# Linear attention and a two-layer ELU network: key projections in 64-row pairs over four banks, zero matmuls in the ramp's gaps, other planned load times and a new fixed order

## The chip, the cores and the metric

One core of one Trainium2 chip. The time is the device time of one launch in microseconds (us); lower is better. A kernel is run several times, and two kernels that are compared run in turn on the same chip. A run that is more than 1.5% above the fastest of the same kernel in its batch is called slow: medians and ranges below include such runs, ratios leave them out. "Span" is the time from the first to the last instruction of one profiled execution; the device time is some 1.8 us longer.

Engines: TensorE does matmuls and transposes, ScalarE the exponentials, VectorE maxima and sums, GpSimd the scaling of the values; GpSimd also issues most of the loads. "Granted clock" is the share of its full clock that the throttle gave TensorE.

## The reference, cut to what matters

```python
# q, k, v: (8 batches, 8 heads, 576 positions, 64); w_phi: (64, 128)
def phi(x):
    proj = einsum('bhsd,df->bhsf', x, w_phi)
    proj = proj - max(abs(proj), axis=-1, keepdims=True)
    return concatenate([exp(proj), exp(-proj)], axis=-1)

q_p, k_p = phi(q), phi(k)
kv  = einsum('bhsf,bhsd->bhfd', k_p, v)
z   = sum(k_p, axis=2)
x   = einsum('bhsf,bhfd->bhsd', q_p, kv) / (einsum('bhsf,bhf->bhs', q_p, z)[..., None] + 1e-6)

x = x.transpose(0, 2, 1, 3).reshape(4608, 512)
h = x @ w_in                                     # w_in: (512, 2048)
g = where(h > 0, h, exp(minimum(h, 0)) - 1)
return g @ w_out                                 # w_out: (2048, 512)
```

## The kernel before

The kernel handles four heads of a batch at a time (a "quad"; 16 in all). For each quad it transposes keys and queries, projects them with `w_phi`, takes exponentials, forms the key-value product (`pkv`), multiplies the queries into it (`pn`), divides, and passes `x` on to the two layers (`ph` is the hidden layer, `po` the output layer). The layers are by far the larger part of TensorE's work.

Nothing is looped in program order. All steps are put down as operations with a cost in us, what they depend on, and how many PSUM banks they take. A planner plays the program through on paper and emits each engine's instructions in the order in which its model started them. What goes first among the ready ones is set by a table of fixed ranks, found by search. So the order is fixed when the kernel is built, and it is as good as the model's numbers are.

The keys before, one step for each bank, on all 128 rows (two 64-row halves beside each other, `w_phi_rhs` is block-diagonal):

```python
def project(n, hh, bank):
    pk = psum(bank, [P, 4, F], FP32, "pk")
    for j in range(2 if hh < 4 else 1):
        nc.tensor.matmul(
            pk[:, 2 * j:2 * j + 2, :].rearrange("p a b -> p (a b)"),
            in_tile(n)[:, 2 * hh + j, :],       # weights
            w_phi_rhs,                          # 128 rows x 256 columns, half of it zeros
            start=True, stop=True)
# ... (cut)
for hh in range(5):
    bank = Bank("first")
    # ... (the exponentials, cut)
    o = add({"PE": 0.22 if hh < 4 else 0.11},
            lambda e, hh=hh, bank=bank: project(0, hh, bank), ..., new=[bank], ...)
```

The queries were already done in the way that the keys get now: two matmuls on 64 rows each, side by side in the array, into two banks.

```python
def project_halves(n, c, pair):
    pk = [psum(bank, [P, 4, F], FP32, f"pk{par}") for par, bank in enumerate(pair)]
    for j in range(4):
        for par in range(2):
            r = slice(par * D, (par + 1) * D)
            nc.tensor.matmul(pk[par][:, j, :], in_tile(n)[r, 4 * c + j, :],
                             w_phi_both[r, par, :], start=True, stop=True)
```

The planner's model of the ramp, and how it gave out banks:

```python
COLD = 20.0            # until then TensorE's costs count times COLD_TIMES
COLD_TIMES = 1.2
CHANGE = 0.095         # a change between 128-row and 64-row matmuls
# ... (cut)
bank.index = min(banks)
```

Of the kernel before, what the change touches and what calls it, by code (L numbers as in the profile page):

```python
# [34 lines left out]
    "020F0U0V0c0a0X0f0b0j0i1E1u1I0l1g1q1o4X3h0n3M3W4j594k580L3J0A01162V4W2W0Z3R0h1U0Y"  # L35
    "2F0+0I1B0Q0-0g560P071b0q181Z0x1y2I0J0T3V1H1p0H381n0S3u1e4z5W3K2M2U323+D9355+4p1J"
    "0E552Z1j0v3700Cp0m3X152S3w0d3r3j061s3p2q6c2m1c453A3H4H0y2O2N0o0N280e1r200M3E4b2n"
    "2r1x0W1t2s1a1l2K0R09121+19102d0k0C2f1z2e11364y2R7n0w535c5g5m313l1X3Y808E8B4V469B"
    "5a5j71C75r6y1k8J2Q42033m0D1CES5D0K9V0G1Y2p1f1S8u4B048V5n4a4c8b3d3B2x5O2P5X0B4I5K"
    "6d9c5M508l0rA3246W1L512cB08zBm30278+AJ2h6e146l3T3e7-5B25E184394D6bAm9-8FEW936j1D"  # L40
    "9Y82AH5q6a8r2y0OEH13I67e9a79B92Y6I5dCC659ICJ8iDy7u4MAGDe9ZB5DGBoErBxFpD+E4DTD5AK"
    "GQDuDl3C3x4Y4A3N263I3OAc235y433U9J3PAN1N8y3yEj4F6R2D1v8Z1A1T225CD7A58K8N5-3ZA-7I"
    "BN773t1Q0p2X8s5s4x4U1w1O1-7z4qAf8j1R2b8e2J6B2z6T3G5Q9M3-5E8Y055N343n3oDp3D6F2l4o"
    "4887215b1G8M4L1F4Z3sBz2w081W5S9z4+3Q7r409u4u6S4e6m1h9v3k4ED4AE4J4s447L4f5p2HA72i"
    "7X7m1dDhB+By2CDD9E4i5T4m6f2B6J7N7Y4R7l9U49Bu9yBL9d5P0uCD5V5H2-BRAY9D6OB-FU4O5F9A"
    "BpA19X3g3L6q4T3i4l880s4G9r4tBk2uDqAsA+3F6o9q5oAq647qCK4w5i2EFF336Q66Iz8W8c8OK98n"
    "J+5fPN2tEq7UPM5e6XAtDi9SBa9pJy1P607THX9RA08AIY2v8d90IOBVE2A4IPB1JE5ZI9ASFo8xBqDz"
    "GjECEuEeE6KcDbQX7vHJFAJgHTEMFRFrEADsN84g543f5A5k6n3q3c6g5w4Q8o6h8U740z2G4h6-6L1m"
    "1i6N3zCt9t7w2A9P3a7VEK6kC-9TD37P8hCPBF8L7SBd8DAe8RCdEZ6z6s8kBT8SCxDA707i7M7Z6Z41"
    "B27fDK635h5I4CCcE0Fq949FBbBI8T6rCb81BeCa8XCOH84-9KDc5Y4N9b6Y0t7E6D2+9h3b17C96A6E"  # L50
    "C49G2j7OCy7j8I4d8G992gDM6V1M97291K6p734P6+2L8QE5EPBD8C9xAxCY9kC81V5z7R7CAwDF4r4S"
    "8t962k5vAADJFGH35JG4B6CsG-62CeEnCRBlM+BA8wCQ52DtC0AhAF5LF8CI6tAPI0Bs6M86CEEE687g"
    "HvEBHO5lPeF0GuALKgDOKxAvKLBvH0AdFMFDIF7ABOCkG+83IDDV8p91QPAgHBAUDgEOH27yApFSHI85"
    "HmCL7B9QO8FjDnD0ITFLLs6uMJJwDRN-FBEyHWLOGJHDNUMMHSH9G6I2FsNAHMIxD-674n3SAi7aBi4K"
    "EmBBDrB372D1CgBQ78BZ9O6iABGKBg75CF9wG9B7EhCzAR8fEsB4AbBM7G69BHCN7sJoCjLWCo4vF+G1"
    "F2ClCvAlFeJpJmGx6CEtCV9HDHC3An8v2o9LL2MXELOJDSEYNnFmDNN7GkDvJhHyG3J49WETEJ47Ex6K"
    "DmBK615R9eAyGnA89iD2DECw6GF96P6HGUEk92Bj95CuCrDxFYC2FnBEFCF47KGOCX9mD8BJAzBXFHCZ"
    "AOA67pHiBSF3EV5tCSCTCMDUG5ChC1BULpGgE+K-DkEpHKGYDYMy7xH6HaJlFzAVBtHCFdHREwFwPUGc"
    "C5AoH+G7L67oPTEFIV5GKVHEM47kLoHQIo7FFkCWFcBrJHDLLaN1ICIRF6H-JuJDM17hRmHqL-FiIXIn"
    "L889LxIwK7AZKPIMLrAkG8JILVGwHVKhKI7dIUP3NFPREvJaLmPuSsQqPWLFHxNhQ7MQElOSMLSwPAQc"  # L60
    "GWI8HHAr2a9N6vFWGm3v9g8PGVFXCAE7CHF7E-7tCfDdEf5xAQF5A2E9FuFT8gGHGAEcDXCnG0BwFf76"
    "BGFyGz6wGrGPGCGIKi7DCUGqCBEiLcFIGDKZFtGXBhAuFlEIHdFVJ7HLMmH1EdNEGZHeNdOIDaOECGHj"
    "N5DoGiIsKeG2Ge9sEN57AIGG8mLNDCGdBY985uF1IgIcCqGaJrLDGRGS6xFx9l9oCmGpEGFPH7FaLI8H"
    "GfBnGv7QAMHGGNAWBcGs8aD6GLHfFZNpLZNwLGLtHFIZGEFhI-DfHZJeIyJnV3I1NbI5JSMuL5JdLuOQ"
    "EaAjH4HYKWP8J8BfHbJfKyIuKDMqMOFJIiJ3Jk9jJLIeM0IqHAE8IKJWPJM5Q4AXT0NXSI7WPXKRTPDI"
    "HzHkJAIWOUJzKkIaKoL+LfJCO6KAJO9CRkJtTS8qLvJjJFLjHUJqIhAaPSQQQ2PfSAPDMHOzPEQfM3S0"
    "OsOlO2P9NLNgNtRRRwPjPpQFOT6U5UDZ9n7bFbGBF-DwK1KBC+ACKUIpKYKrKzKEH5ISLdJKLJP0JQJJ"
    "KsQBLRLKHrKTJ2IrOpN3CiEXC6HhJTQj9+GyI4ItKjJRLXKqKlIEJ5DQL0MBN4JXJZIQOHJ6RnMpNYGF"
    "K+PBJbMnNiHpMGREMKI+SnBPMZK2IIMDMoDWDjEQEgL4INQwKNJGDBOPQmJNL9PzKSJsERHoKtKJIbGt"
    "KXS7QzJBFEFKHcJ9J1NMLAKbJUDPQAEDK3KmMdJVL3K8NzLHO4QMNqQuOGKGLMMYNkKMS3IAQyLzHnOc"  # L70
    "TyIBNmR6J0POMrI7R2IfLUNTMsNCODOyLCHlP5QiLn7JKHNxLEJPJ-NrX47cPdNPMFFNOKRBMlEbIGNj"
    "K59fLyOjWW7+UQPFMN8-U3MTVGGbUpMjWeHtLqPhWcIHILQeWpOmPPPiTVL7GTRHVtA9KnPgX1LlUKPQ"
    "RZQhPKQ8NSPlSuTdT9SoHsV6VKWGVsRAPaU2VBThXOQCOkB8BWGhBCMROgGoK0MkNRO7S4S8SbN0QNJi"
    "QxObOwJcSBNKS5TxOCOeLTTwSJTvU8O1V2R5U9V7LYROT-UoIlT7JvLkO0QLUcIjW5S6MtOONuP6RWRS"
    "JxQbSNLwOMOYNaKfR0MPMfPCMWMhSpMgM2P7M8NOQSUzNvQGO9PmP+FgMvE3EUQUKKLPP2OFKuKdQ6QO"
    "MVV+KpMiJYOqLLOvTEL1SCLeLbV4NZMcSqVXRNOLKwPqIkQERaSzOXKaQHImEzEoTDKQOfLiNGTKPrOo"
    "OhQpOWQsO3RpVpWBRjSxVSRTXGVbR1VmTRRPN9TzRgQ3R7R-NJSyWSJMHNTgXKQ5OdTJTFQRPxRCWJMU"
    "I3QKW+LSTLRuWoOiUgOZPtMaHgSeQ-RDU4ShWqXJUfNoXILhNeVcX8WPSmRtVYP1OASiRMW6TjTQWXO-"
    "U0StWxTGUbSRXLSaUnTnWFWCTeR+PVTcWHVVRIUTOVWDVdVOSTRLUYTBUEV9WaSkONFQFvMSIvVjVgNN"
    "RzMANlMEPySQSGMzSFQrOxSVK6SKSfSgPsSEW0RyT2RsUPKCPkS1NWTuW4RxVxIJS2NVM7RXNyQZVZQY"  # L80
    "GlM6SDVlQ0QTGMUITbQtQWSdOrRQMeMbNcSlUWVTQnWuVUQ1V-VQOuVEVLPIXNTkUCMxKFLgTWSZT4SS"
    "R9U-OBLBO5UAPwNHUXU6P-K4TIRoN6T5SHRfM-QJKvRJN2VhT+SWRlORRbRYLQQaReM9NfOaT3RiRdRV"
    "NBMCTiTmSPViP4QvVPUkNDN+SrV5PvScW2WLPcXDVoTXWAWIPbW7WRSLSjWQVwNQVJULUiSYXEMIU+Rv"
    "VqTsUMR4WgOtHwQdWjIdUOS+VIPGURTMX6WwKOPoX5FOUrTrWtX9TlR3WmUvUqUhX2WVUtV0TUWfVaQk"
    "WzUdUZTfWbSXUmRrWkMwU5RUXCWdUwSOWTWrTZUsVMWZRqSUTATYUuTpPZUyQlVvTCUGQ9UxUaT8W1WM"
    "VyVCPLRcX7NsUVRGW-7HPHVkXFQVUJT6WlWvW3UHWNVHUBS-XAO+U7TtWyATVrV8X0WsUSR8X3UeVDVu"
    "TTXQUDVfXHVFUUVWW9WhW8RFWUQoUNV1XMXPUFTqWiPnWnVRXBU1UjVNVAWKTHSvWORKT1ToPYUlQgTO"
    "VnVeQ+QDOnRhWYSMWETNVzQITa2THPADHuNIS9"
# [37 lines left out]
class Planner:  # L126
# [4 lines left out]
    COLD = 20.0  # L131
    COLD_TIMES = 1.2
# [9 lines left out]
    def __init__(self):  # L142
        self.ops = []
        self.slot = 0.0

# [22 lines left out]
    def run(self):  # L168
        free = dict.fromkeys(self.LAG, 0.0)
        ready = {e: [] for e in self.LAG}  # L170
        banks = set(range(8))
# [61 lines left out]
        while todo:  # L233
            started = False
            for e in ready:
# [22 lines left out]
                for x in o.cost:  # L258
                    ready[x] = [y for y in ready[x] if y[1] is not o]
                for bank in o.new:  # L260
                    bank.index = min(banks)
                    banks.remove(bank.index)
                    held[bank.kind] += 1
                    left[bank.kind] -= 1
                    moe[0] = moe[0] or bank.kind == "ph"
# [4 lines left out]
                if e == "PE" and now < self.COLD:  # L270
                    c *= self.COLD_TIMES
# [17 lines left out]
            for o in [o for o in pending if o.seen <= now]:  # L289
                pending.remove(o)  # L290
                for bank in o.new + o.uses:
                    bank.users -= 1
                    if not bank.users:
                        banks.add(bank.index)
                        held[bank.kind] -= 1
                        started = True
# [13 lines left out]
def kernel(  # L310
# [151 lines left out]
    def plan_quad(i):  # L462
# [32 lines left out]
        for n in range(2):  # L495
# [4 lines left out]
            if i >= DMA_QUAD:  # L500
# [6 lines left out]
                def tail_by_dma(e, n=n, t0=t0):  # L507
# [5 lines left out]
                    {"SP": 1.27}, by_dma, [main, *prior], key=-4.0, load=0.5, alone=1.85  # L513
# [3 lines left out]
                    load=0.15, alone=1.1,  # L517
# [77 lines left out]
        for hh in range(5):  # L595
            bank = Bank("first")


            def exp_k(e, sg, s=None, hh=hh, bank=bank):
                r = slice(0, P) if s is None else slice(s * TAIL, (s + 1) * TAIL)  # L600
                n = 4 if hh < 4 else 2
                nc.scalar.activation(  # L602
                    EK()[:, hh, sg, :] if hh < 4 else EKt[r, s, sg, :],
# [5 lines left out]
            o = add(  # L609
                {"PE": 0.22 if hh < 4 else 0.11},  # L610
                lambda e, hh=hh, bank=bank: project(0, hh, bank),
                [moved[0][0 if hh < 4 else 1], *old("kv")],
                new=[bank],
                key=first + 0.1 * hh if i != 1 else 0.35 + 0.01 * hh,
            )
            ops["k"].append(o)
            m_k.append(
                add(
                    {"DVE": 0.6 if hh < 4 else 0.34},
                    lambda e, hh=hh, bank=bank: reduce(  # L620
                        0,
                        slice(hh // 2 * NS + hh % 2 * NT, hh // 2 * NS + hh % 2 * NT + NT)
                        if hh < 4
                        else TAIL_COLS,
                        bank,
                    ),
# [5 lines left out]
            for sg, s in (  # L632
                ((0, None), (1, None)) if hh < 4 else ((0, 0), (0, 1), (1, 0), (1, 1))
# [3 lines left out]
                        {"ACT": 0.48 if hh < 4 else 0.27},  # L637
# [503 lines left out]
    for c in range(2):  # L1141
        nc.sync.dma_start(out=wst[c * D:(c + 1) * D, :], in_=w_phi)
# [12 lines left out]
    for _ in range(9):  # L1155
        nc.tensor.matmul(warm, zeros[:, 0:P], zeros[:, 0:CHUNK], start=True, stop=True)  # L1156
# [103 lines left out]
```

## Time and profile before

| | before |
|---|---|
| median of 3 runs | 378.59 us (377.31 to 378.9) |
| the profiled run | 375.57 us, span 373.8 us, mean granted clock 0.966 |
| first hidden-layer matmul | 52.9 us |
| TensorE from 10 to 60 us | busy 39.3 of 50 us, granted clock 0.51 to 0.94 |
| ScalarE from 10 to 60 us | busy 47.4 of 50 us |

The profiled run was a lucky draw, 3 us under the median. Single runs of this kernel went from 375.6 to 382.9 us over the whole study, and to 385.4 with the slow ones, so only means of several runs on the same chip are compared below. The table is read as two parts. From the first hidden-layer matmul on, TensorE is full, and the end comes a nearly fixed time later. Before it is a ramp in which loads and four engines share the pace. The lines that carry this stand in the prediction.

### The profile page before, as it was taken

The numbers are of one execution on the slowest core, as the hardware profiler recorded it, in microseconds if no ns is written. First come the engines' busy times: TensorE is split into PE (matmuls) and PEld (weight loads), VectorE is DVE, ScalarE is ACT, GpSimd is POOL, SyncE is SP. The second block draws the span as 40 slices with busy tenths as digits, with TensorE's granted clock in tenths as the row PEclk, the third lists the DMA queues.
The fourth block names the chain that finished last, engine by engine and source line by source line (L and its number), as shares of the span: only waits on it lengthen the run. The fifth ranks groups of instructions, "written<-read, shape, count | busy, mean of one in ns | idle before, by whom it ended". The sixth has DMA issues, their size and how long they took to land.

```text
span 373.8 us, 8380 instructions
## 1 busy us (share of the span) xinstructions
PE 354.6 (95%) x3095; PEld 194.5 (52%) x3095; DVE 267.6 (72%) x558; ACT 274.8 (74%) x604; POOL 247.9 (66%) x359
## 2 busy tenths in 40 slices
PE   6686789999999999999999999999999999999995
PEld 3464664565455654555545546554555554444443
DVE  5789888896897877868875899687978653647000
ACT  3999899899988775986699899977795524656111
POOL 8998959899479558795735871795278733646000
PEclk9578889999999999999999999999999999999999
DMA  8999995999228996589865833761030212000223
GB/s 106 237 252 207 203 179 64 201 190 210 65 49 127 241 209 91 75 133 193 132 77 151 142 55 74 198 168 33 28 89 2 60 43 77 0 30 0 85 61 82
DMA packets 85785, 43.15 MB, mean 115 GB/s; under 512 B 54704, under 2 KB 79664, under 8 KB 85744
## 3 DMA queue, kind: packets, MB, share of 16 engines
q1 hardware_dynamic: 56416, 26.62, 32.5%
q0 software_dynamic: 29328, 16.00, 30.6%
q8 instruction: 24, 0.39, 0.4%
q14 instruction: 17, 0.14, 0.1%
HBM read 36.77 MB, written 9.44 MB: 124 GB/s over the span
## 4 chain that ended last, share of the span: by engine, by line
PE 82%; ACT 9%; DVE 4%; POOL 2%; issue 2%; ACTq 0%; POOLq 0%
PE po L1078 31%; PE ph L1012 29%; PE pkv L783 5%; ACT EK L602 4%; PE pn L831 4%; PE pk L556 4%; PE pk L574 2%; PE tr L528 2%; PE pq L700 2%; ACT EKt L602 1%; ACT Eq L751 1%; PE warm L1156 1%; DVE gT L1035 1%; DVE m_k L583 1%; PE pnt L846 1%
## 5 line engine op out<-in xcount | busy, mean ns | idle before, releaser
L1078 PE MATMUL po<-w_out_sb,gT 128*128 128x512 bf16 (+1 forms) x592 | 136.4, 373 | 0.1
L1028 POOL TENSOR_SCALAR u_sb<-e_sb 128x512 bf16<-128x512 f32 x144 | 88.3, 620 | 55.7 <-ACT e_sb L1024 50.2
L1035 DVE SCALAR_TENSOR_TENSOR gT<-u_sb,ph 128x512 bf16<-128x512 bf16 x144 | 96.1, 683 | 40.1 <-POOL u_sb L1028 39.3
L1012 PE MATMUL ph<-xT,w_in_sb 128*128 128x512 bf16 x512 | 119.3, 379 | 0.8 <-DVE gT L1035 0.7
L1024 ACT ACTIVATE e_sb<-ph 128x512 f32<-128x512 f32 x144 | 86.4, 611 | 38.4 <-PE ph L1012 35.3
L1012 PEld LDWEIGHTS <-w_in_sb 128*128 128x128 bf16 x576 | 54.4, 98 | 63.5 <-issue 4.1
L1078 PEld LDWEIGHTS <-gT 128*128 128x128 bf16 x592 | 55.0, 98 | 57.1 <-issue 4.3
L670 POOL TENSOR_TENSOR vs<-v_b,em 128x512 bf16<-128x512 f32 (+1 forms) x96 | 78.1, 840 | 0.1
L602 ACT ACTIVATE EK<-pk 128x512 bf16<-128x512 f32 x128 | 70.2, 621 | 9.0 <-PE pk L556 7.7
L751 ACT ACTIVATE Eq<-pq 128x512 bf16<-128x512 f32 x128 | 68.4, 614 | 3.4 <-PE pq L700 3.2
L583 DVE TENSOR_REDUCE m_q<-pk 128x4 f32<-128x512 f32 (+1 forms) x80 | 47.8, 629 | 13.0 <-PE pk L574 9.2
L583 DVE TENSOR_REDUCE m_k<-pk 128x4 f32<-128x512 f32 (+1 forms) x80 | 48.5, 631 | 4.1 <-PE pk L556 3.0
L909 POOL TENSOR_TENSOR x<-tot,rec 128x576 bf16<-128x576 f32 x28 | 31.9, 1150 | 16.0 <-DVE rec L905 11.9
L1101 ACT COPY o_sb<-po 128x512 f32<-128x512 f32 (+1 forms) x27 | 15.5, 573 | 35.7 <-PE po L1078 34.4
L866 DVE TENSOR_TENSOR tot<-pn,w 128x260 f32<-128x260 f32 x64 | 26.7, 424 | 8.5 <-PE pn L831 6.3
L831 PEld LDWEIGHTS <-Eq 128*128 128x128 bf16 x512 | 22.9, 98 | 10.4 <-DVE tot L872 1.4
L872 DVE TENSOR_TENSOR tot<-tot,pn 128x260 f32<-128x260 f32 x64 | 26.5, 420 | 0.7
L783 PEld LDWEIGHTS <-EK 128*128 128x128 bf16 x512 | 23.8, 102 | 4.2 <-PE pq L700 0.7
L831 PE MATMUL pn<-kv,Eq 128*128 128x65 bf16 x512 | 25.4, 195 | 0.5 <-DVE qT L536 0.2
L556 PE MATMUL pk<-w_phi_both,kT 128*128 128x256 bf16 x144 | 24.5, 281 | 1.1 <-ACT kv L797 0.4
L602 ACT ACTIVATE EKt<-pk 64x256 bf16<-64x256 f32 x64 | 23.6, 380 | 2.6 <-PE pk L556 2.0
L783 PE MATMUL pkv<-vs,EK 128*128 128x65 bf16 x512 | 25.2, 200 | 0.2 <-DVE m_q L583 0.2
(74 smaller groups left out, 296.2 us busy)
## 6 DMA issues: line engine op xcount, KB each, us to landing
out_dram<-o_sb SPq DMA_DIRECT2D x32, 256.0 KB, 2.5
v_b<-in_v_dram SPq DMA_DIRECT2D x6, 1024.0 KB, 6.4
k_b<-in_k_dram POOLq DMA_DIRECT2D x7, 512.0 KB, 8.1
q_b<-in_q_dram POOLq DMA_DIRECT2D x7, 512.0 KB, 8.7
w_in_sb<-in_moe_w_in_dram POOLq DMA_DIRECT2D x8, 256.0 KB, 7.8
w_out_sb<-in_moe_w_out_dram POOLq DMA_DIRECT2D x4, 512.0 KB, 15.1
v_b<-in_v_dram POOLq DMA_DIRECT2D x2, 512.0 KB, 6.4
v_b<-in_v_dram POOLq DMA_DIRECT2D x1, 1024.0 KB, 11.9
```

Of the source, the lines that this page charges most:

```text
L556: nc.tensor.matmul(pk[:, 2 * j:2 * j + 2, :].rearrange("p a b -> p (a b)"), in_tile(n)[:, 2 * hh + j, :], w_phi_rhs, start=True, stop=True,)
L583: nc.vector.tensor_reduce(largest(n)[:, cols], bank.tile[:, 0:len(range(2 * NS)[cols]), :], axis=AX.X, op=ALU.max, apply_absolute_value=True,)
L602: nc.scalar.activation(EK()[:, hh, sg, :] if hh < 4 else EKt[r, s, sg, :], bank.tile[r, 0:n, :].rearrange("p a b -> p (a b)"), ACT.Exp, sc ...
L670: nc.gpsimd.tensor_tensor(st["vs"][:, sg, r, 0:D], kqv[b, 2][:, o:o + n * D].rearrange("p (n d) -> p n d", d=D), st["em"][:, sg, r, None]. ...
L751: nc.scalar.activation(dst, src, ACT.Exp, scale=1.0 - 2.0 * sg)
L783: nc.tensor.matmul(pkv[:, c, sg, :], st["EK"][:, 2 * c + s, sg, t * F:(t + 1) * F] if t < NT else EKt[:, s, sg, c * F:(c + 1) * F], st["vs ...
L831: nc.tensor.matmul(pt[:, t, :], st["Eq"][:, par, c, sg, o:o + P], st["kv"][:, s, c, sg, :], start=True, stop=True,)
L1012: nc.tensor.matmul(ph, w_in_sb[:, ct, jt * P:(jt + 1) * P], xTs[ch][:, ct, :] if ch < B else xT_tail[:, ct // 2, :, ct % 2, :], start=(ct ...
L1024: nc.scalar.activation(t["e"], bank.tile, ACT.Exp)
L1028: nc.gpsimd.tensor_scalar(t["u"], t["e"], -1.0, 1.0, op0=ALU.add, op1=ALU.mult)
L1035: nc.vector.scalar_tensor_tensor(gTs[ch][:, jt, :], t["u"], 0.0, bank.tile, op0=ALU.min, op1=ALU.max)
L1078: nc.tensor.matmul(bank.tile, gTs[ch][:, jt, tt * P:(tt + 1) * P], w_out_sb[:, jt, o0:o1], start=(jt == 0), stop=(jt == N_JT - 1),)
```

## The change

Its intent: the keys' projection wastes half the array on zeros; the clock is low in the ramp because TensorE has holes there; and the plan's load times don't fit. The diff, without the rank table (all of which is new):

```diff
-    COLD = 20.0
-    COLD_TIMES = 1.2
+    FILL_UNTIL = 60.0
+    FILL = 0.056
@@ the planner starts an operation
+                if e == "PE" and 0.0 < free[e] and now < self.FILL_UNTIL and banks:
+                    n = int(0.5 * (now - free[e]) / self.FILL)
+                    if n:
+                        if filled not in banks:
+                            filled = min(banks, key=banks.get)
+                        self.fill(filled, n)
                 for bank in o.new:
-                    bank.index = min(banks)
+                    bank.index = min(banks, key=lambda j: (j == filled, banks[j], j))
@@ the transposing DMAs (main, tail), for keys and queries and for x
-                    load=0.5       load=0.15
+                    load=0.7       load=0.22
@@ the keys
-        for hh in range(5):
-            bank = Bank("first")
+        main_banks = [[Bank("first") for _ in range(2)] for _ in range(2)]
+        tail_bank = Bank("first")
+        def keys(e):
+            for c in range(2):
+                project_halves(0, c, main_banks[c])
+        for new, c in (((*main_banks[0], *main_banks[1]), None), ((tail_bank,), 2)):
+            o = add({"PE": 0.11 if c else 0.44}, ..., new=new, mode=0 if c else 1, ...)
     (exponentials, maxima and the key-value product use the new order of the rows)
@@ divide
-            den = tile("den", small, [P, 2 * NS], FP32)
+            den = small.tile([P, 2 * NS], FP32, name="den", bufs=2)
@@ the start
-    for _ in range(9):
-        nc.tensor.matmul(warm, zeros[:, 0:P], zeros[:, 0:CHUNK], start=True, stop=True)
+    fill(7, 30)      # thirty 128-column matmuls of zeros
```

## The prediction

> **What bounds the kernel now.** I read the slices of the span first, then stretches of ten and twenty microseconds, then the waits of TensorE, then the chain of waits, and last the order of instructions around single steps.
>
> The slices (each digit is the busy share in tenths of a fortieth of the span, 9.35 us):
>
> ```profile
> PE   6686789999999999999999999999999999999995
> ACT  3999899899988775986699899977795524656111
> POOL 8998959899479558795735871795278733646000
> PEclk9578889999999999999999999999999999999999
> ```
>
> TensorE is full from the seventh slice on and at the full clock. Before that it has holes and a granted clock well below full, while ScalarE and GpSimd are full. So there are two parts: a ramp to about 57 us, and a part in which TensorE alone sets the pace. The stretches put numbers to it (per engine: busy us and instruction count; then the clock, the DMA share and GB/s):
>
> ```profile
> core 0: us, PE busy (x) PEld busy (x) DVE busy (x) ACT busy (x) POOL busy (x), PEclk, DMA share, GB/s
> 10.00:20.00 10.00, 7.13 (x52) 4.99 (x52) 7.28 (x15) 9.67 (x26) 9.55 (x15) 0.51 1.33 231
> 20.00:30.00 10.00, 8.77 (x132) 6.39 (x131) 8.91 (x20) 9.55 (x26) 9.98 (x15) 0.81 1.25 247
> 30.00:40.00 10.00, 6.83 (x85) 4.54 (x85) 9.44 (x21) 9.82 (x25) 8.94 (x13) 0.70 1.31 207
> 40.00:50.00 10.00, 7.04 (x117) 6.13 (x115) 9.03 (x23) 8.74 (x20) 6.35 (x9) 0.84 1.32 187
> 50.00:60.00 10.00, 9.53 (x96) 5.85 (x93) 7.70 (x18) 9.61 (x21) 9.13 (x15) 0.94 1.26 168
> ...
> 200.00:220.00 20.00, 20.00 (x206) 11.02 (x205) 16.08 (x35) 16.92 (x37) 13.30 (x20) 1.00 0.60 129
> ```
>
> From 10 to 60 us TensorE is busy 39.3 of 50 us, so 10.7 us are idle. Busy time times (1 - clock), row by row, gives 3.5 + 1.7 + 2.0 + 1.1 + 0.6 = 8.9 us that it worked longer than at full clock. ScalarE is busy 47.4 of the same 50. From 60 us to the last matmul at 369.5 us TensorE idles about 0.6 us in all (0.11, 0.05, 0.24 and 0.20 in four stretches). A microsecond of TensorE work taken out there comes off the time one for one; one taken out of the ramp does so only where TensorE is what the others wait for. The chain of waits (start, us, what) shows where that is:
>
> ```profile
> 10.92 1.87 PE tr L528 x16
> 12.78 1.41 PE pk L556 x6
> ...
> 19.85 1.71 PE tr L528 x16
> ...
> 38.01 2.36 PE pkv L783 x40
> ...
> 48.39 2.20 PE pkv L783 x40
> ...
> 202.28 1.26 PE pkv L783 x40
> ```
>
> The same 40 matmuls of the key-value product take 2.36 and 2.20 us in the ramp and 1.26 later: the throttled clock lies on the chain.
>
> **What the Trainium skill says.** "TensorE: Matmul & The Clock Gate", Part 1, says the clock is halved by default, that a sustained busy window of about 3.4 us releases it, and that an idle one takes it back. The trace agrees in kind: the mean clock is 0.51 from 10 to 20 us and 1.00 when TensorE is full. Nothing in this trace says how full a window must be, which is the open point about filling half a gap. The same page, Part 3 "Packing small matmuls", says that matmuls on different row groups run at the same time. "TensorEngine Tiling", "Key Properties", says that changing the tiling mode drains TensorE. Both can be measured in a query step, which is already in 64-row pairs:
>
> ```profile
> 161.68 0.29 PE L783 MATMUL pkv<-vs,EK 128*128 128x65 bf16 x4
> 161.80 0.19 PE L783 MATMUL pkv<-vs,EKt 128*128 128x65 bf16 x1
> 161.93 0.40 PE L574 MATMUL pk<-w_phi_both,qT 64*128 64x128 bf16 x8
> 162.16 0.38 PE L700 MATMUL pq<-qT,w_phi_both 64*128 64x512 bf16 x2
> 162.47 1.90 PE L1078 MATMUL po<-w_out_sb,gT 128*128 128x512 bf16 x8
> ```
>
> Eight 64-row matmuls take 162.16 - 161.93 = 0.23 us, so a pair takes 0.058. Groups of five key-value matmuls start 0.158 apart, so the next thing could have started at 161.84; it started at 161.93, 0.09 later. The two wide ones take 0.216 (the pitch of a 512-column matmul), to 162.38; the next starts at 162.47, again 0.09. A change of mode is thus 0.09 us, two per isolated step. "TensorEngine Tiling", Gotcha 1, adds that row tiles running together need different PSUM banks, which is why the new key step takes four banks at once; query steps of this kernel do so already.
>
> **The change part by part.**
>
> 1. Keys. Now: eight 256-column matmuls per quad at 0.107 us (five of them in the full-clock part span 0.71 us with a last one of 0.27, so (0.71 - 0.27)/4 = 0.11), 0.86 us. After: sixteen 64-row, 128-column matmuls in eight pairs at 0.058, 0.46 us. Saved 0.40 per quad; two changes of mode cost 0.18 where the step stands alone, none where it lies beside a query step. Net 0.22 to 0.40. After 57 us the trace has 102 key matmuls, nine to a quad, 11.3 quads. So 11.3 x 0.22 = 2.5 to 11.3 x 0.40 = 4.5 us; I take 3.0, because a step that needs four free banks will seldom be placed right beside another that needs four. The ScalarE, VectorE and key-value counts don't change: the other order of the rows is only followed by other indices.
>
> 2. Zeros in the gaps. The old warm-up of nine 512-column matmuls (4.0 us) becomes thirty of 128 columns; at half clock 30 x 0.107 = 3.2 us, and the first keys land at 5.5 us either way. In the ramp, half of each planned gap is filled at 0.056 per matmul. If the planned idle is like the measured 10.7 us, that is some 5.3/0.056 = 95 matmuls plus a few before 10 us (an estimate). At half clock the same number takes about the whole gap, so TensorE would look full until the clock is released and half full in its gaps after that. I expect the clock from 10 to 60 us to rise from about 0.76 to 0.9 or more. The chain's throttled pieces then shrink: key-value 1.10 + 0.94, transposes 16/16/8 by about 0.9 + 0.8 + 0.4, keys 0.6: 4.7 us. That is the most the clock alone can give. ScalarE has only 50 - 47.4 = 2.6 us of idle in the stretch, so when TensorE gets out of the way ScalarE is next. Of 4.7 I take half, 2.4 us.
>
> 3. Banks are now given out longest-free first rather than lowest number first. That removes some waits for a bank's last reader in the ramp (transposes waited 2.4 us for ScalarE and 1.2 us for VectorE there), though most of these are for data or a true lack of banks. Counted in point 2.
>
> 4. Longer planned transposing DMAs, no planned cold factor, new ranks. No instruction changes its cost by these; only the order does. After 57 us there is nothing to gain in order, since TensorE idles 0.6 us. In the ramp a plan that fits the clock better is worth perhaps 1 us, in the sum. Against this, bursts of four banks of keys (eight exponentials of ScalarE, some 4.5 us to drain) leave less room for the hidden layer: I add back 0.3 us.
>
> Sum: 3.0 + 2.4 + 1.0 - 0.3 = 6.1 us, and from a median of 378.6 that is 372.5. As these new ranks were presumably kept because they paid, I shade it to 372.0 us, 1.7% faster.
>
> **The rivals.**
>
> Rival A: the ramp is ScalarE's and GpSimd's. For it: both are over nine tenths busy through most of 10 to 60 us, and the DMA engines are past their share as well (1.25 to 1.33). Then the warm clock only turns slow TensorE work into idle TensorE time, and all that is left is the keys after 57 us: 378.6 - 3 = 375.6. Against it: the throttled key-value products are on the chain with their full 2.36 and 2.20 us.
>
> Rival B: a shorter latency starts the hidden layer earlier, and everything after gains. The first hidden-layer matmul starts at 52.9 us, right after the copy of the second quad's transposed output. If the chain's 4.7 us come through whole and the new order adds 2, the gain is 3.5 + 4.7 + 2 = about 10 us, 368.5. For it: TensorE has nothing useful to do before that start. Against it: ScalarE's 2.6 us of slack.
>
> Rival C: the new step takes with one hand what it gives. Four banks at once starve the hidden layer of banks, zeros are in the way of real work that comes early, and the fixed order stalls. Then holes of 0.1 to 0.5 us appear in the full part and the time is 376 to 380. Against it: thirty-two query steps of four banks run in the full part today with almost no hole.
>
> **The range and the chances.** A gives 375.6, my sum 372, B 368.5, C above 376. The range 368 to 376 leaves a tenth to each side. The line for faster by over 2% is 378.6 x 0.98 = 371.0, just 1 us below my figure. With a spread of about 3 us I give 0.40 to faster, 0.57 to within, and 0.03 to slower, which only C in a bad form reaches.
>
> **What would show each step right or wrong.** Keys: in the full part, a key step of sixteen matmuls should take 0.46 us start to end with 0.09 before and after; TensorE's work after the ramp should be some 3 us shorter. If the pair's pitch is 0.1 or the change of mode more than 0.09, step 1 is wrong. Clock: the rows from 10 to 60 us should show 0.9 or more, and the first key-value products about 1.3 us; if the clock stays at 0.7 to 0.8, half a gap isn't enough. Ramp: the first hidden-layer matmul should start 2 to 3 us earlier than 52.9. If it starts at 52 or later with a warm clock, A is right; if before 48, B. Idle of TensorE after 60 us should stay under 1.5 us; more means C. The prediction falls if the new order changes what is done in the ramp so much that the start of the hidden layer moves by more than 5 us either way.

## The result, and the profile after

| | before | after |
|---|---|---|
| median | 378.58 us (4 runs, 377.31 to 378.9) | 373.62 us (4 runs, 372.9 to 374.2) |
| span of the profiled run | 373.8 us | 372.0 us |
| mean granted clock in it | 0.966 | 0.995 |
| first hidden-layer matmul | 52.9 us | 51.5 us |

The ratio is 0.9874 [0.9846, 0.9903], 1.3% faster, or 4.8 us of 378.6. A ratio here is the mean time of one kernel's fast runs over that of the other's in the same rounds, so it isn't quite the ratio of the medians; the brackets hold its 95% interval.

The slices after:

```profile
PE   7786988999999999999999999999999999999995
PEclk9999899999999999999999999999999999999999
```

The clock is 9 tenths or more in every slice but the fifth (8), where the second to the sixth were 5, 7, 8, 8 and 8 tenths. The rows of ten microseconds from 10 to 60 us, in the columns that the prediction explained:

```profile
10.00:20.00 10.00, 7.48 (x110) 5.76 (x109) 8.25 (x17) 9.53 (x24) 8.49 (x13) 1.00 1.35 212
20.00:30.00 10.00, 8.77 (x165) 6.79 (x165) 7.97 (x15) 9.93 (x27) 9.31 (x15) 1.00 1.17 192
30.00:40.00 10.00, 6.93 (x124) 5.68 (x121) 8.04 (x20) 6.90 (x19) 9.04 (x13) 0.87 1.21 231
40.00:50.00 10.00, 8.56 (x145) 7.25 (x143) 9.19 (x23) 9.61 (x23) 9.63 (x12) 0.96 1.35 207
50.00:60.00 10.00, 9.84 (x110) 5.31 (x110) 8.22 (x18) 9.57 (x22) 8.86 (x15) 1.00 1.40 224
```

The clock averages (1.00 + 1.00 + 0.87 + 0.96 + 1.00)/5 = 0.97, with its lowest row at 0.87. But TensorE's busy time is no less than before, since zeros are counted as work, and the hidden layer starts only 1.4 us earlier. The chain of waits says what the ramp is made of now (start, us, what):

```profile
5.54 7.16 DMA k_b<-in_k_dram
...
25.17 10.60 DMA q_b<-in_q_dram
...
36.90 1.69 PE pkv L797 x40
...
45.71 3.54 ACT EK L629 x7
...
50.20 13.69 DMA k_b<-in_k_dram
```

Three loads account for 31 us of the first 64 us of this chain. Only one long piece of the key-value product is left on it there. The waits of TensorE (total us, times, longest) agree:

```profile
PE tr L537 <- DMA k_b<-in_k_dram: 2.5, 2, 1.2
PE trt L541 <- DMA q_b<-in_q_dram: 1.9, 1, 1.9
```

The new key step stands here between two parts of the output layer:

```profile
77.52 1.03 PE L1097 MATMUL po<-w_out_sb,gT 128*128 128x512 bf16 x4
78.49 0.62 PE L583 MATMUL pk<-w_phi_both,kT 64*128 64x128 bf16 x16
79.04 3.63 PE L1097 MATMUL po<-w_out_sb,gT 128*128 128x512 bf16 x16
```

Four wide matmuls at a pitch of 0.216 end at 78.38 and the keys start at 78.49. From there to the next matmul it is 0.55 us: eight pairs at 0.058 make 0.46, and the change of mode makes 0.09. (The 0.62 of the record runs to the modelled end of the last matmul.) From one output part to the next it is 79.04 - 77.52 = 1.52 us. And the zeros:

```profile
L1247 PE MATMUL fill<-zeros 128*128 128x128 bf16 x212 | 20.4, 243 | 3.1 <-DVE zeros L1163 1.0 <-DVE tot L885 0.9 <-ACT EK L629 0.6
```

212 matmuls, 30 at the start and 182 in gaps. At a pitch of 0.056 those in the gaps fill some 10 us.

### The profile page after: what moved, and what is told of

It is laid out like the page before. It is cut to its first block, busy times and chain, and to the rows that moved or that the text cites. A ratio compares the mean times of both kernels' runs of the same rounds, so it can differ in the third digit from the quotient of the medians.

```text
span 372.0 us, 8975 instructions
## 1 busy us (share of the span) xinstructions
PE 352.5 (95%) x3380; PEld 197.1 (53%) x3426; DVE 266.9 (72%) x562; ACT 271.8 (73%) x601; POOL 248.3 (67%) x359
## 4 chain that ended last, share of the span: by engine, by line
PE 76%; DMA 8%; POOL 6%; ACT 4%; issue 3%; DVE 1%; POOLq 0%; ACTq 0%
PE po L1097 33%; PE ph L1031 27%; DMA k_b<-in_k_dram 6%; PE pkv L797 4%; PE pk L583 4%; PE pn L850 3%; DMA q_b<-in_q_dram 3%; POOL u_sb L1047 2%; POOL vs L684 2%; PE pq L714 1%; ACT EK L629 1%; POOL w_in_sb L385 1%; PE pnt L865 1%; ACT EKt L629 1%; DVE gT L1054 1%
## 5 line engine op out<-in xcount | busy, mean ns | idle before, releaser
L1097 PE MATMUL po<-w_out_sb,gT 128*128 128x512 bf16 (+1 forms) x567 | 130.8, 373 | 1.6 <-issue 0.6
L1047 POOL TENSOR_SCALAR u_sb<-e_sb 128x512 bf16<-128x512 f32 x144 | 88.0, 618 | 49.4 <-ACT e_sb L1043 46.4
L1031 PEld LDWEIGHTS <-w_in_sb 128*128 128x128 bf16 x576 | 53.6, 98 | 62.0 <-issue 4.2
L1097 PEld LDWEIGHTS <-gT 128*128 128x128 bf16 x592 | 54.0, 98 | 56.9 <-issue 2.9
L629 ACT ACTIVATE EK<-pk 128x512 bf16<-128x512 f32 x128 | 68.6, 628 | 11.9 <-PE pk L583 11.5
L765 ACT ACTIVATE Eq<-pq 128x512 bf16<-128x512 f32 x128 | 69.9, 622 | 3.2 <-PE pq L714 3.1
L891 DVE TENSOR_TENSOR tot<-tot,pn 128x260 f32<-128x260 f32 x64 | 25.7, 420 | 0.4
L797 PEld LDWEIGHTS <-EK 128*128 128x128 bf16 x512 | 22.3, 98 | 3.3 <-PE fill L1247 0.2
L797 PE MATMUL pkv<-vs,EK 128*128 128x65 bf16 x512 | 23.8, 195 | 0.1
L1247 PE MATMUL fill<-zeros 128*128 128x128 bf16 x212 | 20.4, 243 | 3.1 <-DVE zeros L1163 1.0
```

The lines of the kernel that those rows point to most:

```text
L629: nc.scalar.activation(EK()[:, 2 * c + par, sg, :] if c < 2 else EKt[r, s, sg, :], bank.tile[r, 0:n, :].rearrange("p a b -> p (a b)"), ACT ...
L765: nc.scalar.activation(dst, src, ACT.Exp, scale=1.0 - 2.0 * sg)
L797: nc.tensor.matmul(pkv[:, c, sg, :], st["EK"][:, 2 * c + t % 2, sg, (2 * s + t // 2) * F:(2 * s + t // 2 + 1) * F,] if t < NT else EKt[:, ...
L1031: nc.tensor.matmul(ph, w_in_sb[:, ct, jt * P:(jt + 1) * P], xTs[ch][:, ct, :] if ch < B else xT_tail[:, ct // 2, :, ct % 2, :], start=(ct ...
L1047: nc.gpsimd.tensor_scalar(t["u"], t["e"], -1.0, 1.0, op0=ALU.add, op1=ALU.mult)
L1097: nc.tensor.matmul(bank.tile, gTs[ch][:, jt, tt * P:(tt + 1) * P], w_out_sb[:, jt, o0:o1], start=(jt == 0), stop=(jt == N_JT - 1),)
```

## The experiments

All kernels computed the reference's result. Medians of "before" in the four batches of runs, each on another chip, were 377.4, 378.9, 378.4 and 381.0 us, so the ratio to it is the number to compare.

### The kernel before again, and with the zeros alone

`b_again` is the unchanged kernel, to see how much it moves by itself. There is no edit.

> The kernel before once more, for a second trace of it. Its first profiled run took 375.57 us, its timed runs 377.3 to 378.9. Theory (throttle): the ramp of the kernel before depends on when the clock is released and taken back, so its runs scatter, and a run of 378 to 379 us will show a mean clock below the 0.966 of the first trace (0.95 or so) and more slow TensorE work before 57 us. Rival (chance elsewhere): the same clock within 0.005, and the 3 us lie after 60 us.

379.06 us (378.09 to 382.8), ratio 1.0042 [0.9958, 1.0126]. Its profiled run had a span of 378.1 us, 4.3 more than the first profile of the same kernel, at the same clock (0.964 against 0.966), and its first hidden-layer matmul came at 55.5 us instead of 52.9. The row from 30 to 40 us of this run, and a piece of its chain of waits:

```profile
30.00:40.00 10.00, 5.03 (x51) 2.83 (x51) 8.63 (x21) 9.23 (x23) 7.65 (x12) 0.71 1.36 186
```

```profile
19.14 14.09 DMA v_b<-in_v_dram
```

The second batch's values, issued at 19.1, landed at 33.2 us; in the first profile they landed at 31.1. I had thought that the scatter of this kernel came from the throttle. Between these two profiles it does not: the clock in this row is 0.71 where it was 0.70 before. Nor do the 4.3 us lie after 60 us, as the rival had it: 2.6 of them come before the hidden layer and 1.7 after its start. The chain points to the landing of this load, which no run changed by itself. Two profiles don't clear the throttle in general, but over the 32 fast runs of the kernel before in the four batches time and mean clock go together only weakly (correlation -0.24).

`b_fill` puts only the zeros into the kernel before, with its own order and keys (and with the two buffers of `den`).

```diff
+                if e == "PE" and 0.0 < free[e] and now < self.FILL_UNTIL and banks:
+                    n = int(0.5 * (now - free[e]) / self.FILL)
+                    ...
+                        self.fill(filled, n)
-    for _ in range(9):            # the old warm-up
+    fill(7, 30)
```

> The kernel before with its order and its key steps, but the gaps planned before 60 us half filled with zeros (166 small matmuls, and 30 in place of the warm-up). Theory (throttle): clock from 10 to 60 us near 1, 375.0 to 376.5 us, so 2 to 3.5 us faster than before. Rival (ScalarE and GpSimd bind the ramp): the clock rises as much, but the time stays within 1 us of 378.6. Rival (zeros in the way): slower than before.

379.21 us (377.26 to 380.1), ratio 1.0021 [0.9948, 1.0094]: nothing gained. The rows of its ramp, and a wait of TensorE:

```profile
10.00:20.00 10.00, 7.13 (x97) 5.61 (x95) 8.05 (x16) 9.88 (x27) 8.77 (x15) 1.00 1.33 229
20.00:30.00 10.00, 8.94 (x154) 6.70 (x152) 8.70 (x20) 10.00 (x26) 9.98 (x14) 1.00 1.24 247
30.00:40.00 10.00, 8.51 (x146) 6.63 (x143) 8.93 (x20) 9.30 (x24) 8.93 (x13) 1.00 1.38 201
40.00:50.00 10.00, 7.23 (x101) 6.27 (x99) 9.00 (x23) 8.36 (x19) 6.91 (x10) 0.85 1.29 201
50.00:60.00 10.00, 9.77 (x119) 7.21 (x119) 5.61 (x13) 7.28 (x17) 6.35 (x10) 0.81 1.29 158
```

```profile
PE fill L1239 <- ACT kT L547: 2.2, 1, 2.2
```

The clock went from 0.51, 0.81 and 0.70 to 1.00 in the first three rows, and the first hidden-layer matmul came at 55.9 us, about as late as in `b_again`. From 20 to 30 us ScalarE and GpSimd are busy for 10.00 and 9.98 of 10 us, so a faster TensorE had nothing to gain from them there. In the last two rows, just ahead of the hidden layer, the clock is no higher than before (0.85 and 0.81 against 0.84 and 0.94), so this run tests a warmer clock only up to some 40 us; the next one tests more. The second fence shows a small price. A zero matmul into a bank has to wait for that bank's last reader, 2.2 us in this one case.

### The changed kernel without one of its parts

`a_nofill` leaves the zeros in the gaps out of the changed kernel; the order of everything else stays.

```diff
-                    n = int(0.5 * (now - free[e]) / self.FILL)
+                    n = 0
```

> The changed kernel with the same order and banks, only the 182 zeros in the gaps left out (the first 30 stay). Theory (throttle): the clock of the ramp falls to 0.7 to 0.85, 375.5 to 377 us, so 2 to 3 us slower than the changed kernel (373.6). Rival (ramp bound elsewhere): within 1 us of 373.6.

373.53 us (372.94 to 375.37), ratio 0.9874 [0.9797, 0.9951], against 0.9874 with zeros. The clock did fall back, to 0.50, 0.60, 0.74, 0.84 and 0.73, 0.68 on average where it was 0.97:

```profile
10.00:20.00 10.00, 6.06 (x55) 4.09 (x56) 7.15 (x15) 7.73 (x20) 8.30 (x13) 0.50 1.35 217
20.00:30.00 10.00, 9.36 (x115) 6.33 (x115) 7.47 (x16) 9.93 (x27) 9.52 (x16) 0.60 1.15 177
```

In the profiled run, the slowest of the five, the first hidden-layer matmul came at 53.7 us instead of 51.5; the median doesn't show that loss. So a clock of 0.50 to 0.84 in this ramp costs nothing that these runs can tell from zero. The interval is wide (this run's ratio alone is uncertain by 0.8%, 3 us), so it takes the other two comparisons with and without zeros, `b_fill` above and `d_tails_nofill` below, to say so.

`a_keys256` keeps the order, the four-bank step and the zeros, but does the keys as before with eight 256-column matmuls on 128 rows.

```diff
         def keys(e):
             for c in range(2):
-                project_halves(0, c, main_banks[c])
+                for par in range(2):
+                    project(0, 2 * c + par, main_banks[c][par])
     (and the old order of the rows in the maxima and the key-value product)
```

> The changed kernel with the same order and the same four-bank step, but the keys' projections made of eight 256-column matmuls on all 128 rows again. Counted from the instruction order, TensorE's work after the first hidden-layer matmul grows by 5.4 us of matmuls less 24 changes of mode of 0.09 us, 3.2 us. Theory (TensorE alone binds after the ramp): 376.5 to 377.2 us, 3.2 us slower than the changed kernel. Rival (the pairs are hidden or the changes of mode cost more than 0.09): within 1.5 us of 373.6.

376.11 us (375.69 to 376.48), ratio 0.9946 [0.988, 1.0011]. That is a little under the 376.5 to 377.2 that was expected. None of its four runs reaches any of `a_nofill`'s five in the same batch. The pairs are thus worth 0.9946 - 0.9874 = 0.72% of 378.6, 2.7 us, by the ratios of this kernel and the changed one; the plain means of this kernel and `a_nofill`, 376.10 and 373.70, say 2.4, but these two differ in the zeros as well. The same place of the program as above shows it in one step:

```profile
77.11 1.03 PE L1093 MATMUL po<-w_out_sb,gT 128*128 128x512 bf16 x4
77.98 1.04 PE L565 MATMUL pk<-w_phi_both,kT 128*128 128x256 bf16 x8
78.86 3.62 PE L1093 MATMUL po<-w_out_sb,gT 128*128 128x512 bf16 x16
```

From one output part to the next it is 78.86 - 77.11 = 1.75 us, with no change of mode; with pairs it was 1.52. An isolated step saves 0.23 us. In this order twelve quads have their keys after the start of the hidden layer (192 of the 64-row matmuls in the changed kernel's trace), and 12 times 0.23 is 2.8.

`a_order` goes one step further: 256-column keys, no zeros in gaps, and the lowest free bank again. What is left of the change is the new ranks, with the load times and the one-step keys that they were planned for, and two small things: the thirty zeros in place of the warm-up and the two buffers of `den`.

```diff
     (a_keys256, and)
-                    n = int(0.5 * (now - free[e]) / self.FILL)
+                    n = 0
-                    bank.index = min(banks, key=lambda j: (j == filled, banks[j], j))
+                    bank.index = min(banks)
```

> The changed kernel's order alone: keys in 256-column matmuls on all rows, no zeros in gaps, lowest free bank first. If neither zeros nor banks are worth anything, it stands where the 256-column kernel stood, 375.5 to 376.7 us, and what is left against the kernel before (about 2 us) is the order's. If the bank policy matters, it is slower than that, 377 us or more. If the zeros and the warm clock matter only together with slow key steps, the same: 377 or more.

376.66 us (375.4 to 377.05), ratio 0.9944 [0.9898, 0.9989], the same as `a_keys256`. So zeros and bank order together make a difference of 0.02% between the ratios, far inside the intervals, and the order alone is worth 0.56%, or 2.1 us, with an interval from 0.4 to 3.9. 2.7 and 2.1 make the whole 4.8; that is no check of the two, since both were taken as differences along one path from the kernel before to the changed one.

### What sets the ramp: the loads

With the clock ruled out, my next theory was that the landings of single loads set the start of the hidden layer, so that a better order of loads should give more. For the next four kernels the planner's list is collected, some loads on GpSimd change places with each other, and the rest is emitted as it was.

`d_qtail` issues the second batch's query tails (the wait of 1.9 us above) five transfers earlier.

```diff
+    def edit(emit):      # the places of these loads in GpSimd's list, in this order
+        permute(emit, [(1, 1, 0), (1, 1, 1), ("w_in", 1, 0), ("w_in", 0, 3),
+                       ("w_in", 0, 2), ("w_in", 0, 1), (1, 2, 0)])
```

> The changed kernel with one small load, the second batch's query tails, issued on GpSimd right after that batch's queries in place of five transfers later (the six others move down by one place). Nothing else changes on any engine. Theory (loads pace the ramp): the tails land 5 to 7 us before the 35.8 us of the changed kernel, TensorE's wait of 1.9 us for them goes, the first hidden-layer matmul starts 1 to 1.9 us before 51.5, and the time falls to 371.7 to 372.8 us. Rival (ScalarE binds the ramp): the wait goes, and the time stays within 0.5 us of 373.6.

373.85 us (372.93 to 375.54), ratio 0.9861 [0.981, 0.9913]. The mechanism works and the gain is gone. The tails landed at 24.8 us instead of 35.8, that wait vanished, and the first hidden-layer matmul came at 49.7 instead of 51.5. Then this:

```profile
64.01 0.23 PE L545 MATMUL trt<-ident,k_b 128*128 128x128 bf16 x1 [2.66 <-DMA k_b<-in_k_dram]
...
64.34 3.55 PE L1035 MATMUL ph<-xT,w_in_sb 128*128 128x512 bf16 x8
```

The key tails of the third batch land at the same time as before, and TensorE, now ahead, stands 2.66 us where it had stood 0.83 (the number in brackets is the idle time). The next eight hidden-layer matmuls run at half clock, 3.55 us, where eight took 1.89 at the full one. 1.8 us of wait plus 1.7 of slow clock are 3.5, more than the 1.8 that were won, and this profiled run is indeed the slowest of the five, 375.54 us. The other four, at 372.93 to 374.05 us, show mean clocks of 0.993 to 0.999 against its 0.992; whether they had the slow stretch isn't shown. The added wait alone would cancel the gain.

`d_lift` adds to this an earlier second half of the very first keys.

```diff
+        permute(emit, [(0, 0, 0), (0, 0, 2), (0, 0, 1), (0, 1, 0), (0, 2, 0)])
```

> As d_qtail, and the second half of the first batch's keys is also issued second in place of fifth (the first values fifth). Theory (loads pace the ramp): these keys land near 9 in place of 12.7 us, TensorE's wait of 1.2 us there goes too, 0.3 to 1.2 us faster than d_qtail. Rival: the early values are missed now, or ScalarE has no room: as d_qtail or slower.

376.1 us (372.95 to 376.78), ratio 0.9919 [0.9856, 0.9981]. These keys landed at 8.2 us, but the queries and values that they had passed landed later, at 11.6 and 13.9, and waits for query loads of 2.6 us came up. Further on, its profile has the same stop as that of `d_qtail`: 2.74 us of waiting for the third batch's key tails, to 65.3 us. It is not better than `d_qtail`, and its four runs scatter too much to say that it is worse.

`d_tails` adds to `d_qtail` that the third batch's keys and their tails go ahead of two loads of `w_out` and of the fourth batch.

```diff
+        permute(emit, [(2, 0, 0), (2, 0, 1), ("w_out", 2), (3, 1, 0),
+                       (3, 0, 0), ("w_out", 3), (3, 0, 1)])
```

> As d_qtail, and the third batch's keys and their tails issued right after the second batch's value tails, ahead of two output-weight loads and the fourth batch's keys and queries (a permutation of seven loads on GpSimd, nothing else). In d_qtail the hidden layer started 1.8 us earlier, and the gain was lost again at 61 to 68 us: a wait of 2.7 us for these key tails (landed at 64.0), and eight hidden-layer matmuls after it at half clock (3.4 in place of 1.7 us). Theory (loads pace the ramp, one landing after another): the tails land near 50 us, both losses go, 369.3 to 371.5 us. Rival (ScalarE binds): within 1 us of 373.6, with the wait moved to ScalarE or VectorE.

373.59 us (372.52 to 375.18, six runs), ratio 0.9887 [0.9846, 0.9928]. The key tails landed at 49.4 instead of 64.0 us and the wait for them is gone. In its place:

```profile
PE pq L718 <- DVE m_k L596: 1.9, 1, 1.9
PE tr L984 <- DVE x L932: 1.8, 1, 1.8
```

```profile
40.00:50.00 10.00, 6.02 (x103) 4.92 (x100) 9.96 (x18) 8.51 (x20) 8.08 (x10) 0.93 1.40 205
```

VectorE is busy 9.96 of 10 us, and the first hidden-layer matmul is at 53.2 us, later than without the edit. A load taken off the path put another engine there.

`d_tails_nofill` is the same without zeros in gaps (`n = 0`), in case a clock matters once the loads don't.

> d_tails without the zeros in the gaps. If loads were what hid the clock's worth, then with the loads out of the way the zeros are worth something: 1 to 3 us slower than d_tails. If the clock of the ramp is worth nothing in any case: within 0.7 us of it.

374.09 us (371.77 to 376.29), ratio 0.9894 [0.9844, 0.9943], 0.07% from `d_tails` in the same batch. The zeros show no worth here either.

`d_more` issues each load of `w_out` twice, to see what more bytes in the ramp cost.

```diff
     def load_w_out(jt):
+        for _ in range(2):
             nc.gpsimd.dma_start(out=w_out_sb[:, jt:jt + 4, :], in_=w_out_r[:, jt:jt + 4, :])
```

> The changed kernel with each of the four loads of the output weights issued twice (27 to 45 us into the span), same data. Theory (the ramp is paced by when loads land): in the changed kernel two such loads land 2.5 us apart, so everything queued behind slips by up to 10 us; the time rises by 4 us or more, and TensorE waits for loads of keys and queries between 35 and 75 us. Rival (ScalarE and GpSimd bind the ramp): only the 3.2 us that GpSimd takes to issue four more, mostly hidden: under 1.5 us slower.

408.19 us, ratio 1.0803 [1.0725, 1.0881]. This experiment is confounded and says nothing on bandwidth: the second write of a tile had to wait for the landing of the first, on the engine that issues both.

```profile
POOL w_out_sb L392 <- DMA w_out_sb<-in_moe_w_out_dram: 27.5, 3, 11.6
```

GpSimd stood 27.5 us, and the first hidden-layer matmul moved from 51.5 to 85.9 us. One thing can be used: the start moved by 34.4 us and the median by 34.6. A later start of the hidden layer was paid one for one here.

### New searches

`tuned_a` and `tuned_b` tell the planner that the first batch's loads take 1.25 times and the values 1.4 times as long, as the landings suggested, each with a table of ranks from a search of its own over the planned end.

```diff
+        if name[0] == 0:
+            landed[name].load *= 1.25
+        (values: *= 1.4; and new ranks)
```

> The changed kernel with the planned bytes of the first batch's loads raised by 25% and of the later values by 40% (as the trace's spacing of landings asks), and ranks searched anew for that. Theory (a plan that lands its loads when the chip does loses less to waits in the ramp): TensorE's waits for loads before 70 us under 1 us in all (5 us in the changed kernel), and 370 to 372 us. Rival (ScalarE, VectorE, GpSimd and loads are all near full there, so a wait taken away comes back as another): the waits for loads go, and the time stays within 1 us of 373.6.

> The same plan with the ranks of another search from the same start. The same expectations; if the two differ by more than 1.5 us, the outcome of a search is chance at this size and a gain of one of them proves nothing about the loads.

`tuned_a` took 385.53 us (382.63 to 389.11), ratio 1.0164 [1.0097, 1.0231]; `tuned_b` 377.27 (374.8 to 381.95), ratio 0.9904 [0.9834, 0.9974]. Two searches with the same numbers differ by 8 us, so neither result tells anything on these numbers. Nor did the waits for loads go: before 70 us TensorE waited 4.6 and 2.6 us for them, against 5.2 in the changed kernel, where under 1 was expected. In `tuned_a` the zeros themselves waited 9.7 us, mostly for readers of their bank (3.0 in the changed kernel); whether that made the start late wasn't tried. None of the versions tried beats the changed kernel by more than the noise.

### All profiles side by side

| profiled run | first hidden-layer matmul, us | span, us | span minus start, us |
|---|---|---|---|
| before | 52.9 | 373.8 | 320.9 |
| b_again | 55.5 | 378.1 | 322.6 |
| b_fill | 55.9 | 378.1 | 322.2 |
| a_order | 53.0 | 375.3 | 322.3 |
| a_keys256 | 52.1 | 374.0 | 321.9 |
| after | 51.5 | 372.0 | 320.5 |
| a_nofill | 53.7 | 373.6 | 319.9 |
| d_tails | 53.2 | 373.1 | 319.9 |
| d_tails_nofill | 52.5 | 371.2 | 318.7 |
| tuned_a | 61.5 | 380.9 | 319.4 |
| tuned_b | 54.6 | 373.0 | 318.4 |
| d_more | 85.9 | 406.6 | 320.7 |
| d_qtail | 49.7 | 373.8 | 324.1 |
| d_lift | 50.9 | 375.0 | 324.1 |

The first five rows have 256-column keys and need 321 to 323 us after the start. The next seven have pairs and need 318 to 321, on average 2.3 us less. The last two started earliest and needed 324: in both, TensorE then stood some 2.7 us for one load.

## Why the prediction was right or wrong

The predicted time was 372.0 us in a range of 368 to 376, with "within 2%" the likeliest at 0.57. Measured were 373.6 us and -1.3%. The total came out right, but its terms did not all do so, and errors of opposite sign helped it; that part is luck.

**Step 1, keys: right, mechanism and size.** It put 3.0 us on them, from 0.22 to 0.40 per quad. Measured were 2.7 us by the ratios of two kernels that differ in nothing else, 2.4 against one that also lacks the zeros, and 0.23 us in an isolated step, the lower end. The pitch of 0.058 and the change of mode of 0.09 were both met. One reading was loose: a pair needs two banks, and the new step takes four because both of its halves are planned as one operation.

**Step 2, zeros in the gaps: the step that failed.** Its first half held: the clock rose from about 0.76 to 0.97 where "0.9 or more" was expected. Its second half, "Of 4.7 I take half, 2.4 us", gave nothing that shows: 1.0021 for the zeros in the old kernel, 0.9874 with or without them in the new one, 0.07% in a third order. 2.4 us would be 0.63%; each comparison alone is uncertain by that much or a little more, but none of the three shows more than 0.07% in that direction. That throttled products lay on the chain of waits was read as "they cost their extra time". A chain shows who came last, not what would come last if that one were faster. ScalarE, at 47.4 of 50 us, and loads in flight for 10 to 14 us are what the traces offer as next in line; that they, and which of them, held the start is argued from the traces, not shown. Rival A had said this of ScalarE and GpSimd. The count was off as well: 182 zero matmuls in gaps, not 95. At 0.056 us each and half filled they stand for at least 20 us of planned gaps, where I had taken the 10.7 us of idle time measured before. The start of the hidden layer was to come 2 to 3 us before 52.9; it came 1.4 before.

**Step 3, banks:** counted in step 2, and with it nothing: the kernel with neither zeros nor the new bank order has the ratio 0.9944 against 0.9946 with both. They were only taken away together, and with 256-column keys.

**Step 4, order: undersized.** It put 1.0 us on a better plan and took 0.3 for bursts of four banks. Measured were 2.1 us, between 0.4 and 3.9, for the order with its load times and one-step keys. What the profiles show of it is little: the first hidden-layer matmul of the kernel with the order alone came at 53.0 us, where the two profiles of the kernel before have 52.9 and 55.5. Its four runs lie between 375.4 and 377.05 us, those of the kernel before on the same chip between 375.69 and 380.01, and one slow one at 382.41, so a part of the 2.1 us may be fewer bad draws; four runs are too few to show that. What of the 2.1 us is due to the ranks and what to the new planned load times was not tried apart.

**The sum.** 2.7 + 2.1 + 0 = 4.8 us, against 3.0 + 2.4 + 1.0 - 0.3 = 6.1. The zeros were too large by 2.4 and the order, 0.7 net, too small by 1.4: by chance these made up for each other in part.

**The rivals.** A was right that the clock was worth nothing and wrong on the total (375.6), since it gave the order nothing; the start that was to mark it, 52 us or later, was missed by half a microsecond (51.5). B (368.5) falls: the start came 1.4 us earlier, not 10, and where it came 1.8 us earlier still, in `d_qtail`, nothing more was gained. C's sign was idle time of TensorE after 60 us of more than 1.5. By the records the changed kernel has 4.5 us of it against 0.6 before, but most of that is no idleness: its trace has 2668 matmuls against 2709 weight loads from 60 us on, so some 40 records are missing, where the trace before has them all. Waits over 0.15 us with a named cause are two, 0.83 and 0.47 us, and `d_tails`, with the same key step and no record missing, has 0.3 us in all. So C doesn't show. (The prediction counted 32 query steps in the full part; after 57 us there are 26, the rest lie in the ramp.)

**What stays open:** what the ramp would be worth with all of its loads in time, why `d_lift` was no faster than `d_qtail`, and why one of the two searches starts its hidden layer 10 us later than the changed kernel.

## What to carry to other kernels

In a part where one engine is full to the end, price a change in that engine's instructions by the step between its neighbours: 0.23 us there, times the count, gave 2.8 us where 2.4 to 2.7 were measured. In this ramp, where loads and three engines are all nearly full, a wait removed came back as another, and a faster clock for the engine that waits showed no worth; in one like it, try it with one edit before counting on it. Where the order comes from a search over a model, the order itself is a part of the change worth microseconds, and has to be measured as one.

## What the Trainium skill lacked or had wrong

- "TensorE: Matmul & The Clock Gate", Part 1, says that about 3.4 us of sustained work release the clock and an idle window of as much takes it back, and doesn't say how full a busy window must be. Half-filled planned gaps held the clock at 1.00 from 10 to 40 us in the kernel with zeros alone, and not throughout: it was 0.81 from 50 to 60 us. The busy share alone doesn't decide: from 10 to 20 us TensorE was busy 7.13 of 10 us both in the kernel before and in that one, at a clock of 0.51 and 1.00. And in `d_qtail` an idle time of 2.66 us was followed by eight 512-column matmuls at half speed, 3.55 us against 1.89, so less than 3.4 us of measured idleness cost the clock there (just before it lay 0.6 us of transposes; whether these count as work the trace doesn't tell, and without them it would be about 3.3).
- "TensorEngine Tiling", "Key Properties", says that a change of tiling mode drains TensorE and gives no figure: 0.09 us here, each way.
- I found no page that gives a figure for how long a small load takes behind larger ones: the query and key tails took 10.6 and 13.7 us from issue to landing in the ramp.
- I found no page that warns that a warming matmul waits for the last reader of its bank: 2.2 us once in the kernel with zeros alone.
